# Row statistics of the last spectral tiles moved to where the rows are made, and other places for steps of the attention

## The chip, the cores and the metric

The kernel runs on one core of a Trainium2 chip. The time is device microseconds of that core, the median of the runs shown. Its engines appear under the profile's names: PE is the matrix engine (PEld its weight loads), DVE the vector engine, ACT the scalar engine with the exponentials, POOL the general engine, and SP issues the transfers.

## The reference, cut to what matters

Four layers work on `x` of 2048 rows and 512 columns in f32, each as `x + layer(layernorm(x))`: a spectral layer, an attention layer, then both once more.

```python
def spectral(x):
    a = einsum("bsd,ed->bse", x, dft_hid_re); b = einsum("bsd,ed->bse", x, dft_hid_im)
    return einsum("ts,bse->bte", dft_seq_re, a) - einsum("ts,bse->bte", dft_seq_im, b)

def attention(x, wq, wk, wv, wo, beta):      # 32 heads of 16, 4 segments of 512 rows
    for s in range(4):
        p = softmax(qs @ ks.T * scale + causal_mask)
        a_mem = (phi(qs) @ M) / (phi(qs) @ z + 1e-6)   # memory of the segments before
        o = g * a_mem + (1 - g) * (p @ vs)
        M = M + phi(ks).T @ vs;  z = z + sum(phi(ks))  # phi(t) = t + 1 for t > 0, else exp(t)
    return concat(o) @ wo
```

Both layers begin with a layernorm, which needs a mean and a variance of each row of what the layer before wrote.

## The kernel before, in words

Rows are worked in 16 tiles of 128 rows (`tt`, `i`), four to a segment. The program is the two spectral layers and the two attentions, woven together at their seams. Between them, x goes through DRAM tiles `mid`.

**The spectral layer** multiplies the normalised rows with the DFT matrices (tiles `m`, then `u`, then `y`), the matrices streamed from HBM into a ring (`cring`). Where row tiles are finished, `finish` (L234) adds the residual into `xr` and writes `mid`. For the first three quarters of the rows `measure` (L267) then takes the mean and the variance (`moments`, L195, the statistics at L197) from `xr`, which is still in the chip. When the four tiles of a segment are measured, it turns the variances into row scales: `ve` on DVE, a power on POOL (L210), three small DVE steps `rt` and `row_r` (L215 to L218). The last four tiles, of segment 3, are finished by `hidden_last` (L648), which measures nothing; `prep` of segment 3 reads them back (`xt<-mid`, L185) and does the same statistics there, in the middle of the attention.

**The attention** goes through 32 units, 8 to a segment, 4 heads each (units 0 to 31 in the first attention, and the second attention's are counted 32 to 63 here). A unit has these pieces:

- `nat`: score tiles with rows on the partitions, in pieces of 512, 128+384, 512, 128+384 and 256 columns. DVE takes the maxima of their rows (`junk`, `mx`, L969) and makes `mparts`; PE transposes these (`mT`), ACT copies them (`mt`), and a transfer puts them beside the stacked q (`stkq<-mt`, L1007), so that the next score product subtracts them.
- `sT`: transposed score tiles; ACT reads them (`sT`, L1040; `pT`, L1043 with the exponential), POOL masks the diagonal (L1046).
- `pv_bank`: the value products, 32 columns of PE at a time, at the beginning of a unit as the trace shows it.
- `on`, `oT`: the output transposed to rows and, per row tile, back to columns (`transpose_out`), copied out by ACT and DVE (`oh`, L141).
- `pm` and `pM`, `pkT`: reading the memory (`mem_read`; DVE then does `den`, L1177 and L1185, and `onat`, L1187) and updating it (`mem_update`).
- projections (`pqk`, `pvv`) of the next segment and the output projection (`po`) of the segment before. These run as pairs of half-height products: two tiles, a fixed number of steps apart, each using 64 of PE's rows (`chain_step`). Each unit has 24 of these steps, and `WIN` spreads them over three stretches of the unit.

All PSUM tiles of one bank come from a ring of eight, so a new one waits until the tile of eight before has been read.

**What sets the order.** Each piece is a generator. `place(order, gen, times)` (L250) puts it into a table of slots; ten slots make a unit. At the end the table is worked off by time and then by `order`, and each step records its instructions. PE's order is exactly this program order. On DVE, ACT, POOL and SP a scheduler chooses with the program order as priority; the maxima are given a higher priority. The table's numbers are constants at the top of the file: `S_AT` for the `sT` steps, `N_AT` for `nat`, `PV`, `TO` and `TURN` for value products, output and maxima; `WIN` for the pairs; `ORDER` for the tile that joins each place of the chain; `OT_AT`, `PREP_AT`, `READ_AT`, `UPA` and `UPB` for the unit of a segment in which a transpose, a normalisation, a memory read and the two halves of an update come. The first and the last segment have numbers of their own (`_FIRST`, `_LAST`), and `NL0` says from which unit of the last segment `nat` goes by the last segment's. `ROWS_AT` are the slots in which the second spectral layer loads and normalises its rows, relative to its start.

Of the kernel before, what the change touches and what calls it, by code (L numbers as in the profile page):

```python
# [22 lines left out]
NSEG = 4  # L23
# [4 lines left out]
LT = L // P  # L28
# [13 lines left out]
VW = DH + 1  # L42
HALF = NT // 2
URGENT = 150
S_AT = (1.0, 2.5, 3, 6.0, 7.5)
N_AT = (-17, -15.05, -12, -10.95, -8.0, -8)
PV = 11.05
PVF = 12
W = 2.5
TURN = -5  # L50
TO = 0.8
TURNED = (12.5, 12.5, 14)
WIN = ((4.1, 9), (6.1, 7), (8.1, 8))
LAGS = 18
ORDER = "k3 q3 o1 o0 o2 o3 k0 q0 v2 q1 k1 k2 v1 q2 v3 v0"
OT_AT = (1, 1, 1, 2)
PREP_AT = (2, 3)
READ_AT = (0, 3, 5, 7)
UPA = (-1, 3, 5, 7)
UPB = (4, 4, 6, 8)  # L60
ORDER_FIRST = "q3 k3 - - - - v2 k0 q0 k2 q1 k1 v1 q2 v3 v0"
PREP_FIRST = (2, 3)
UPA_FIRST = (1, 2, 4, 7)
UPB_FIRST = (2, 7, 8, 8)
ORDER_LAST = "k3 q3 o2 o0 - o3 - o1 - - - - - - - -"
OT_LAST = (1, 3, 1, 1)
READ_LAST = (1, 3, 5, 6)
NL0 = 1
SL0 = 2
TURN_LAST = -5  # L70
TURNED_LAST = (12.5, 12.5, 14)
TO_LAST = 1.9
ROWS_AT = (-32, -24, -6, 2, 26, 26, 46, 66)
S_LAST = (0.5, 2.5, 3, 6.0, 7)
N_LAST = (-16.5, -14.05, -13, -11.5, -10.4, -8)
PV_LAST = 10.5
OWO = 0.8
OWU = 0.6
OWP = 0.3
OWR = 0.2  # L80
OWB = 0.3
STK = -21.5
# [15 lines left out]
def spectral_infini_kernel(  # L98
# [155 lines left out]
    def run_from(t, n, step=1):  # L254
        return range(t, t + n * step, step)
# [18 lines left out]
    def place_spectral(x_in, x_out, t0, end, ln_at, direct):  # L274
# [373 lines left out]
        def hidden_last(tcn):  # L648
# [18 lines left out]
            for tt in range(LT):  # L667
                finish(ps[tt], xr[tt], x_out, tcn * LT + tt)
            yield

        for n, t in ln_at:
            measured = t - (1.5 if n[0] == HALF and direct else 3)
# [64 lines left out]
        for tcn in range(TC):  # L737
            if tcn == 0:
                at = [end + k // 2 for k in range(nh)]
            elif tcn < TC - 1:  # L740
                at = [end + nh // 2 + ((tcn - 1) * nh + k) // 3 for k in range(nh)]
            else:
                at = run_from(end + nh // 2 + 2 * nh // 3 + 1, 2 * DT, 2)
            for tt in range(LT):
                place(3.7, split_u(tcn, tt), [at[tt * 2 * DT if tcn < TC - 1 else 0] - 4])
            place(4, (hidden if tcn < TC - 1 else hidden_last)(tcn), at)

    def place_attention(x_in, x_out, t0, w_at, out_at):
# [3 lines left out]
        def prep(s, n):  # L752
# [1 line left out]
            yield  # L754
            mine = slice(s * LT + n[0], s * LT + n[-1] + 1)
            mv, rr = row_mv[:, mine], row_r[:, mine]
            if s == NSEG - 1:
                ve, r = row_stats(xt, mv)
            yield
            if s == NSEG - 1:  # L760
                row_scale(rr, ve, r)
                yield
            xn = []
            for j, i in enumerate(n):
                with behind_max():
# [580 lines left out]
        for s in range(NSEG):  # L1346
            b = t0 + SS * s
            for j in range(2):
                t = b - 43 + 5 * j if s == 0 else apart(s - 1, (PREP_AT if s > 1 else PREP_FIRST)[j])
                first = (12, 10, 6, 4, 3) if s == NSEG - 1 else (11, 8, 5, 3) if s else (8, 5, 4, 3)  # L1350
                place(OWP, prep(s, (2 * j, 2 * j + 1)), [*(t - d for d in first), t, t + 1] if s == 0 else [*(t - d for d in first), t])
            if s == 0:
                place(2, values(s), run_from(b - 18, 8), light(b - 10))
                chain.update({k - 4: chain_proj(0, 2, n) for k, n in ((2, "q"), (3, "k"))})
            at = 2 * USEG * s
            for i in range(LT):
                if s > 0:
# [2 lines left out]
            for name in (ORDER_FIRST if s == 0 else ORDER if s < NSEG - 1 else ORDER_LAST).split():  # L1360
                n, i = name[0], int(name[1:] or 0)
                if n == "-":
                    order.append(None)
                elif n == "o":
                    order.append(chain_out(s - 1, i))
                elif n == "v":
                    order.append(chain_values(s + 1, i))
                else:
                    order.append(chain_proj(s + (i < 3), i, n))
            chain.update({at + h: tile for h, tile in enumerate(order) if tile})  # L1370
# [154 lines left out]
```

## Time and profile before

| | |
|---|---|
| median of three runs | 1778.73 us (1775.21 to 1781.76) |
| profiled execution, and its span | 1775.0 us, 1773.2 us |
| PE busy | 1723.8 us, 97% |
| DVE, ACT, POOL busy | 74%, 62%, 28% |
| mean granted clock of PE | 0.990 |
| first spectral layer, to about | 470 us |
| first attention | 475 to 914 us |
| second spectral layer, to about | 1345 us |
| second attention | 1345 us to the end |

"Busy" of PE is modelled from pipelined matmuls, so a PE that is busy by the page may still work slower than it could. The page's clock line gives the granted clock in tenths. A row of busy time by stretch gives the stretch in us, its length, and for each engine the busy time and the number of instructions, then the granted clock, the share of the transfer engines in use and the rate in GB/s.

### The profile page before, as it was taken

The page shows a single profiled execution, that of the slowest core. Times are in us where ns is not written, and L with a number is a line of the kernel's source. Part 1 is how long each engine was busy: PE and PEld are TensorE (multiplying, and loading weights), DVE is VectorE, ACT ScalarE, POOL GpSimd, SP SyncE. Part 2 cuts the span into 40 slices and gives each one's busy share as a digit, 9 for nine tenths or more (in the row PEclk, how much of TensorE's full clock was granted, in tenths as well). Part 3 has the DMA queues.
Part 4 walks back from the last instruction along what each step waited for, and adds up shares of the span by engine and source line. Part 5 has one row for each costly group of instructions (what it writes and reads, how often), then busy time and mean ns, then how long its engine had stood idle before and what let it go on. Part 6 is the DMA issues. An engine that isn't in the chain of part 4 may idle for free.

```text
span 1773.2 us, 35306 instructions
## 1 busy us (share of the span) xinstructions
PE 1723.8 (97%) x11504; PEld 1341.4 (76%) x11504; DVE 1314.6 (74%) x3949; ACT 1095.5 (62%) x2452; POOL 489.5 (28%) x769
## 2 busy tenths in 40 slices
PE   8999999999999999999999999999999999999998
PEld 6888777877668777777678878888876777777775
DVE  8888978863676876868877997667637667677685
ACT  3344443532588888787764666444418887987885
POOL 1000000003236465455410000000034544754542
PEclk9999999999999999999899999999999999999999
DMA  8787774355455554665656877554555446546551
GB/s 285 248 274 236 250 243 167 103 178 166 125 150 147 134 145 119 159 154 132 178 188 204 277 226 241 193 165 125 171 162 161 123 109 163 146 120 161 135 141 36
DMA packets 145511, 303.29 MB, mean 171 GB/s; under 512 B 18096, under 2 KB 22192, under 8 KB 145328
## 3 DMA queue, kind: packets, MB, share of 16 engines
q1 hardware_dynamic: 138416, 288.44, 54.9%
q10 hardware_dynamic: 6912, 12.59, 1.9%
q8 instruction: 93, 1.52, 0.4%
q14 instruction: 90, 0.74, 0.2%
HBM read 211.83 MB, written 88.08 MB: 169 GB/s over the span
## 4 chain that ended last, share of the span: by engine, by line
PE 78%; DVE 12%; ACT 4%; issue 3%; DMA 2%; POOL 0%; SPq 0%; DVEq 0%; ACTq 0%; POOLq 0%
PE m L124 26%; PE pqk L124 9%; PE y L124 8%; PE pv_bank L124 8%; PE nat L124 5%; PE u L124 5%; PE pvv L124 5%; PE po L124 4%; PE sT L124 4%; DVE junk L969 2%; DVE c L591 2%; DVE clo L141 1%; ACT pT L1043 1%; PE pM L124 1%; PE on L124 1%
## 5 line engine op out<-in xcount | busy, mean ns | idle before, releaser
L969 DVE CUSTOM_DVE_ANT_0 junk<-nat,mask 128x128 bf16<-128x128 f32 (+3 forms) x896 | 368.9, 457 | 231.6 <-PE nat L124 217.4
L1043 ACT ACTIVATE pT<-sT 128x512 f32<-128x512 f32 x640 | 353.1, 607 | 3.3 <-DVE sT L1038 1.1
L124 PE MATMUL m<-chi,xa 128*128 128x512 f32 x1056 | 308.3, 392 | 2.4 <-DVE c L591 2.1
L1046 POOL TENSOR_SCALAR_AFFINE_SELECT pT<-pT 128x256 f32<-128x256 f32 (+1 forms) x448 | 193.2, 446 | 399.8 <-ACT pT L1043 329.3
L124 PE MATMUL m<-clo,xa 128*128 128x512 f32 x720 | 231.8, 394 | 4.7 <-DVE clo L141 4.4
L124 PEld LDWEIGHTS m<-chi,xa 128*128 128x128 f32 x1056 | 198.0, 188 | 47.0 <-DVE c L591 2.9
L1040 ACT ACTIVATE sT<-sT 128x256 f32<-128x256 f32 x625 | 181.8, 329 | 80.4 <-PE sT L124 74.8
L124 PE MATMUL nat<-stkk,stkq 48*128 48x384 f32 (+3 forms) x1024 | 197.3, 354 | 12.3 <-PE sT L124 3.4
L124 PE MATMUL pqk<-xT,wq 64*128 64x512 f32 (+1 forms) x720 | 193.7, 399 | 0.8 <-ACT pT L1043 0.6
L124 PE MATMUL pqk<-xT,wk 64*128 64x512 f32 (+1 forms) x720 | 188.3, 398 | 0.3
L124 PE MATMUL y<-wdt,us 128*128 128x512 f32 x768 | 182.3, 391 | 0.2 <-DVE wdt L141 0.2
L124 PE MATMUL pvv<-wv,xT 64*128 64x512 f32 (+1 forms) x672 | 173.2, 402 | 0.5 <-DVE xT L141 0.4
L124 PEld LDWEIGHTS nat<-stkk,stkq 48*128 48x128 f32 x1024 | 122.6, 187 | 65.8 <-ACT pT L1043 19.3
L124 PE MATMUL sT<-stkq,stkk 50*128 50x256 f32 (+3 forms) x1024 | 165.6, 334 | 5.9 <-DMA stkq<-mt 2.7
L124 PEld LDWEIGHTS y<-wdt,us 128*128 128x128 f32 x768 | 143.4, 188 | 30.5 <-DVE wdt L141 0.9
L124 PEld LDWEIGHTS m<-clo,xa 128*128 128x128 f32 x720 | 134.7, 188 | 37.8 <-DVE clo L141 8.9
L124 PE MATMUL pv_bank<-pT,v_all 128*32 128x512 f32 (+3 forms) x2048 | 162.5, 452 | 0.2 <-DVE xr L235 0.2
L139 ACT ACTIVATE chi<-cring 128x512 fp32r<-128x512 f32 (+1 forms) x138 | 99.7, 727 | 88.0 <-PE m L124 40.1
L210 POOL TENSOR_TENSOR r<-ve,half_neg 128x2 f32<-128x2 f32 (+2 forms) x24 | 19.7, 819 | 481.3 <-DVE ve L208 457.5
L124 PE MATMUL po<-wo,oh 64*128 64x512 f32 (+1 forms) x672 | 147.7, 401 | 1.1 <-ACT oh L139 0.5
L124 PEld LDWEIGHTS pqk<-xT,wq 64*128 64x128 f32 (+1 forms) x720 | 123.9, 187 | 13.4 <-issue 2.2
L124 PEld LDWEIGHTS sT<-stkq,stkk 50*128 50x128 f32 x1024 | 105.5, 188 | 37.3 <-issue 12.4
(191 smaller groups left out, 3134.5 us busy)
## 6 DMA issues: line engine op xcount, KB each, us to landing
cring<-in_ct SPq DMA_DIRECT2D x97, 256.0 KB
scrk<-parts SPq DMA_DIRECT2D x96, 256.0 KB
stkq<-scrq SPq DMA_DIRECT2D x128, 192.0 KB
stkk<-scrk SPq DMA_DIRECT2D x128, 192.0 KB
cring<-sum SPq DMA_DIRECT2D x95, 256.0 KB
xt<-mid SPq DMA_DIRECT2D x64, 256.0 KB
scrq<-parts SPq DMA_DIRECT2D x32, 512.0 KB
cring<-in_ct SPq DMA_DIRECT2D x27, 512.0 KB
```

The lines of the kernel that those rows point to most:

```text
L124: return tc.keep_in_program_order(op(*args, **kwargs))
L139: pin(A.activation(hi, src, AF.Copy, scale=scale))
L141: lo_engine.tensor_tensor(out=lo, in0=src, in1=hi.bitcast(F32), op=ALU.subtract)
L210: G.tensor_tensor(out=r, in0=ve, in1=half_neg[:, :n], op=ALU.pow)
L591: V.tensor_tensor(out=dst, in0=c[tcn, base][:, m], in1=ps[m], op=op)
L969: last_max[0] = V.tensor_tensor_reduce(trash, src, mask[:, 512 - n :], 1.0, 3e38, ALU.add, ALU.min, dst,)
L1040: done = A.activation(blocks, blocks, AF.Relu)
L1043: A.activation(dst[a], ps, AF.Exp, scale=-SCALE)
L1046: G.affine_select(blocks, blocks, pattern=[[0, n] for n in blocks.shape[1:-1]] + [[1, P]], compare_op=ALU.is_ge, fill=0.0, base=0, channel ...
```

## The change

The last spectral tiles are measured in `hidden_last`, in four steps that are placed after its end, and `prep` of segment 3 does no statistics any more: the four `moments` per seam go from `xt` to `xr`, and their scales are made once for four tiles rather than twice for two. The two projections ahead of the chain are named by a constant `ORDER_PRE`, and `ORDER` may now name tiles "Q" and "K", which none of the lists does. All else are numbers of the table. Lines of the changed file stand one further from L43 on.

```diff
-S_AT = (1.0, 2.5, 3, 6.0, 7.5)
-N_AT = (-17, -15.05, -12, -10.95, -8.0, -8)
-PV = 11.05
+S_AT = (1.0, 2.5, 3, 5.5, 7.5)
+N_AT = (-16.05, -15.1, -12.05, -10.95, -8.0, -8)
+PV = 11.9
...
-TO = 0.8
+TO = 0.75
-WIN = ((4.1, 9), (6.1, 7), (8.1, 8))
+WIN = ((4.1, 10), (6.1, 6), (8.1, 8))
...
-READ_AT = (0, 3, 5, 7)
-UPA = (-1, 3, 5, 7)
-UPB = (4, 4, 6, 8)
-ORDER_FIRST = "q3 k3 - - - - v2 k0 q0 k2 q1 k1 v1 q2 v3 v0"
+READ_AT = (1, 3, 5, 7)
+UPA = (-1, 3, 3, 7)
+UPB = (4, 5, 6, 8)
+ORDER_PRE = "q2 k2"
+ORDER_FIRST = "q3 k3 - - - - v2 k0 q0 q1 k1 k2 v0 q2 v3 v1"
...
-UPA_FIRST = (1, 2, 4, 7)
+UPA_FIRST = (1, 2, 4, 5)
...
-OT_LAST = (1, 3, 1, 1)
+OT_LAST = (1, 2, 1, 1)
...
-NL0 = 1
+NL0 = 0
...
-TO_LAST = 1.9
-ROWS_AT = (-32, -24, -6, 2, 26, 26, 46, 66)
-S_LAST = (0.5, 2.5, 3, 6.0, 7)
-N_LAST = (-16.5, -14.05, -13, -11.5, -10.4, -8)
-PV_LAST = 10.5
+TO_LAST = 0.8
+ROWS_AT = (-38, -24, -12, 2, 26, 28, 40, 66)
+S_LAST = (1.5, 2.5, 3, 6.0, 6)
+N_LAST = (-15.55, -14.05, -12.5, -11.0, -10.9, -8)
+PV_LAST = 11.5
...
-OWP = 0.3
+OWP = 0.4
...
             for tt in range(LT):
                 finish(ps[tt], xr[tt], x_out, tcn * LT + tt)
             yield
+            for tt in range(LT):
+                measure(tcn, tt, xr[tt])
+                yield
...
                 at = run_from(end + nh // 2 + 2 * nh // 3 + 1, 2 * DT, 2)
+                at = [*at, *(at[-1] + 4 + k for k in range(LT))]
...
-            if s == NSEG - 1:
-                ve, r = row_stats(xt, mv)
-            yield
-            if s == NSEG - 1:
-                row_scale(rr, ve, r)
-                yield
+            yield
...
-                first = (12, 10, 6, 4, 3) if s == NSEG - 1 else (11, 8, 5, 3) if s else (8, 5, 4, 3)
+                first = (11, 8, 5, 3) if s else (8, 5, 4, 3)
...
-                chain.update({k - 4: chain_proj(0, 2, n) for k, n in ((2, "q"), (3, "k"))})
+                for k, name in enumerate(ORDER_PRE.split()):
+                    if name != "-":
+                        chain[k - 2] = chain_proj(0, 2, name[0].lower())
...
+                elif n in "QK":
+                    order.append(chain_proj(s, i, n.lower()))
```

What this does to the order of the instructions shows at three places.

DVE in unit 17, where statistics for segment 3 stood before; the rows begin behind the four maxima of 256 columns.

```order
L1133 TENSOR_TENSOR rec<-on,gate 128x16
L988 TENSOR_SCALAR mparts_70<-mx 128x2x8
L1139 RECIPROCAL rec<-rec 128x16
L989 SCALAR_TENSOR_TENSOR mparts_70<-mx,mparts_70 128x2x8
L197 BN_STATS st<-xt 128x6
L1150 TENSOR_TENSOR ot<-on,rec 128x256
L198 BN_AGGR row_mv<-st 128x2
L197 BN_STATS st<-xt 128x6
L141 TENSOR_TENSOR oh<-oT,oh 128x512 x2
L969 ISA junk,mx<-nat,mask 128x512
```

The same place of the changed kernel:

```order
L1177 SCALAR_TENSOR_TENSOR den<-pm,gate 128x16
L988 TENSOR_SCALAR mparts_70<-mx 128x2x8
L1177 SCALAR_TENSOR_TENSOR den<-pm,gate 128x16
L989 SCALAR_TENSOR_TENSOR mparts_70<-mx,mparts_70 128x2x8
L1185 RECIPROCAL den<-den 128x32
L1133 TENSOR_TENSOR rec<-on,gate 128x16
L1187 TENSOR_TENSOR onat<-pm,den 128x2x128 x2
L1139 RECIPROCAL rec<-rec 128x16
L142 TENSOR_TENSOR oh<-oT,oh 128x512
L1150 TENSOR_TENSOR ot<-on,rec 128x256
L142 TENSOR_TENSOR oh<-oT,oh 128x512 x2
L969 ISA junk,mx<-nat,mask 128x512
```

The statistics are gone from here; the work of the memory read (`den`, `onat`) and the third `oh` now stand ahead of the maximum of the first 512 columns.

PE at the beginning of unit 8 before, where the first memory read of segment 1 stood:

```order
L124 MATMUL nat<-stkk,stkq 128x256 x4
L124 MATMUL sT<-stkq,stkk 128x384 x2
L124 MATMUL sT<-stkq,stkk 128x128 x2
L124 MATMUL pm<-state_4422,phi 128x136 x4
L124 MATMUL pM<-v_all,pkn 128x136 x8
L124 MATMUL on<-ident,ot 128x128 x4
```

and at the beginning of unit 9 in the changed kernel:

```order
L125 MATMUL nat<-stkk,stkq 128x256 x4
L125 MATMUL sT<-stkq,stkk 128x384 x2
L125 MATMUL sT<-stkq,stkk 128x128 x2
L125 MATMUL pm<-state_4443,phi 128x136 x4
L125 MATMUL on<-ident,ot 128x128 x4
L125 MATMUL oT<-ident,onat 128x128 x12
```

The read stands one unit later, ahead of the three transposes of the output. The same holds for units 16 and 17, 40 and 41, 48 and 49.

SP near the end of the first attention, around the transfer of the transposed maxima (`stkq<-mt`), before:

```order
L416 DMA cring<-in_ct 128x512 x2
L236 DMA mid_9_140<-xr 128x512
L416 DMA cring<-in_ct 128x512 x6
L185 DMA xt<-mid_8_139 128x512
L1007 DMA stkq<-mt 2x8x128 x2
L185 DMA xt<-mid_9_140 128x512
L185 DMA xt<-mid_10_141 128x512
```

and changed:

```order
L417 DMA cring<-in_ct 128x512 x4
L237 DMA mid_9_140<-xr 128x512
L417 DMA cring<-in_ct 128x512 x4
L186 DMA xt<-mid_8_139 128x512
L186 DMA xt<-mid_9_140 128x512
L186 DMA xt<-mid_10_141 128x512
L1007 DMA stkq<-mt 2x8x128 x2
```

Two loads of spectral rows have come ahead of it.

## The prediction

> **What bounds the kernel now.** I read the page from the top: busy shares, slices in time, the chain.
>
> ```profile
> span 1773.2 us, 35306 instructions
> PE 1723.8 (97%) x11504; PEld 1341.4 (76%) x11504; DVE 1314.6 (74%) x3949; ACT 1095.5 (62%) x2452; POOL 489.5 (28%) x769
> PEclk9999999999999999999899999999999999999999
> PE 78%; DVE 12%; ACT 4%; issue 3%; DMA 2%; POOL 0%; SPq 0%; DVEq 0%; ACTq 0%; POOLq 0%
> ```
>
> PE is the bound: busy 1723.8 of 1773.2 us, and 78% of the chain. All its idle time is 49.4 us, and the change removes no matmul, so it can win only idle time, time at a lower clock, and matmuls that are stretched by what they wait for. So I compared units of one kind in the view of busy time by stretch (length; busy us of PE, PEld, DVE, ACT, POOL, each with its count; clock; DMA share; GB/s): three output units of segment 2 beside those of segment 3, in attention 1 and 2, and behind them the same four stretches for L197, the statistics of a row tile, alone.
>
> ```profile
> 581.86:625.91 44.05, 42.56 (x403) 32.17 (x406) 37.44 (x135) 34.31 (x86) 19.80 (x33) 1.00 0.51 140
> 695.34:741.40 46.06, 42.93 (x402) 30.84 (x406) 40.05 (x153) 35.26 (x86) 21.34 (x35) 1.00 0.52 135
> 1453.60:1497.60 44.00, 42.51 (x402) 32.06 (x406) 34.82 (x131) 34.33 (x86) 19.80 (x33) 1.00 0.52 141
> 1566.84:1612.99 46.15, 42.53 (x403) 31.78 (x406) 38.51 (x151) 35.06 (x87) 21.46 (x35) 1.00 0.51 132
> ...
> 581.86:625.91 44.05, 2.50 (x4) 1.00 0.51 140
> 695.34:741.40 46.06, 5.16 (x8) 1.00 0.52 135
> 1453.60:1497.60 44.00, 0.00 (x0) 1.00 0.52 141
> 1566.84:1612.99 46.15, 2.69 (x4) 1.00 0.51 132
> ```
>
> PE has the same number of matmuls in all four, yet units 17 to 19 and 49 to 51 take 2.01 and 2.15 us longer than units 9 to 11 and 41 to 43. What they have beyond the others is four statistics of xt (2.69 us, 0.67 each) and what hangs on them: `prep` of segment 3 computes its row scales there, because the rows come too late for the segment before. The chain of waits runs through that work in unit 17 and again in unit 18 (start, us):
>
> ```profile
> 704.81 0.74 POOL r L210
> ...
> 706.62 0.51 DVE rt L217
> ...
> 707.87 0.50 PE sT L124
> ...
> 718.46 0.60 DVE st L197
> ...
> 720.36 0.58 DVE st L197
> ```
>
> DVE works in its order; the maxima (junk) that free the banks of `nat` stand behind these pieces, and PE waits for a bank.
>
> **The change, part by part.** The sum is made against the profiled execution's 1775.0 us.
>
> *Row statistics where the rows are made.* The statistics leave units 17 to 19 and 49 to 51. If these then run as their twins, that is −2.01 −2.15 = **−4.1**. Bounds: no gain, if the pace was set by something else there, and −4.1. The twins have the same PE instructions, so I take −4.1.
>
> The four statistics go to the lead of each attention, where the last row tiles are finished. The first row is DVE's busy time in the lead, the second the first maximum after it, with the idle time ahead of it:
>
> ```profile
> 446.70:458.58 11.88, 5.87 (x30) 1.00 0.41 140
> ...
> 458.58 0.69 DVE L969 CUSTOM_DVE_ANT_0 junk<-nat,mask 128x512 bf16<-128x512 f32 x1 [4.89 <-PE nat L124]
> ```
>
> DVE is idle for 4.89 us just where the moved work (4×0.67 = 2.7 and small pieces) comes. Without that cover PE would wait for the maxima: +2.7 in the first lead. The order puts the first statistic between maxima that PE waits for, so I take one of the four as uncovered: **+0.6**, bounds 0 and +2.7.
>
> *First memory read from units 8, 16, 40, 48 to 9, 17, 41, 49.* In units 8 and 16 nothing of it is hidden, PE is dense there; in 9 and 17 PE waits later for the transposed output. Unit 25 already has the order that unit 9 now gets: read, `on`, twelve `oT`. So I compare both from the value products to the first `po`, PE's timeline first, then the chain in unit 25, then DVE's timeline in unit 9:
>
> ```profile
> 570.23 1.19 PE L124 MATMUL pm<-state,phi 128*128 128x136 f32 x8
> 571.26 2.02 PE L124 MATMUL pM<-v_all,pkn 128*128 128x136 f32 x16
> ...
> 581.79 2.36 PE L124 MATMUL pv_bank<-pT,v_all 128*32 128x512 f32 x32
> ...
> 588.46 0.47 PE L124 MATMUL po<-wo,oh 64*128 64x512 f32 x1 [0.20 <-DVE mx L969]
> ...
> 807.15 2.36 PE L124 MATMUL pv_bank<-pT,v_all 128*32 128x512 f32 x32
> ...
> 814.29 0.50 PE L124 MATMUL po<-wo,oh 64*128 64x512 f32 x1
> ```
>
> ```profile
> 811.77 0.75 DVE onat L1187 x2
> ...
> 813.63 0.61 DVE oh L141
> ```
>
> ```profile
> 587.63 0.68 DVE L969 CUSTOM_DVE_ANT_0 junk<-nat,mask 128x512 bf16<-128x512 f32 x1
> ...
> 588.23 1.28 DVE L141 TENSOR_TENSOR oh<-oT,oh 128x512 fp32r<-128x512 f32 x2
> ```
>
> The read takes 571.26 − 570.23 = 1.03 us of PE and leaves unit 8. In unit 9 the way to the first `po` is 588.46 − 581.79 = 6.67 us, in unit 25 it is 814.29 − 807.15 = 7.14, though unit 25 has no `nat` of 256 columns there. So the read adds at least 0.47 in its new place. It adds more where those tiles stand too, since DVE then comes from their maxima, does `onat` (0.75) and `oh`, and only then lets `po` start; I take 0.9 of the 1.03. Four units times −0.13 is **−0.5**; the end on the good side is 4×−1.03 = −4.1 (wholly hidden), the bad one is the fourth rival's.
>
> *Output transpose from unit 27 to 26, `nat` steps of units 22 to 25 and 54 to 57 in the order of the last units, earlier spectral rows.* Rows of busy time by stretch: units 22 to 25, 26 to 28, 29; then two windows of 3.41 us at the half-clock piece, and one for comparison.
>
> ```profile
> 768.49:822.12 53.63, 53.42 (x528) 41.05 (x532) 38.82 (x172) 45.35 (x115) 27.46 (x46) 1.00 0.52 133
> 822.12:859.10 36.98, 34.99 (x292) 24.97 (x293) 32.20 (x126) 28.43 (x76) 23.26 (x38) 0.95 0.61 157
> 859.10:872.23 13.13, 9.71 (x83) 6.02 (x86) 12.87 (x58) 9.50 (x26) 4.91 (x10) 0.89 0.98 286
> ...
> 838.75:842.16 3.41, 2.64 (x15) 1.69 (x14) 3.31 (x12) 3.41 (x10) 3.33 (x4) 1.00 0.43 122
> 842.16:845.57 3.41, 3.41 (x19) 2.91 (x19) 2.45 (x11) 2.68 (x7) 2.23 (x7) 0.50 0.33 117
> 698.80:702.21 3.41, 2.40 (x19) 1.75 (x17) 3.41 (x16) 3.41 (x9) 1.64 (x4) 1.00 0.00 0
> ```
>
> Units 22 to 25 have 0.21 us of idle PE, so their new order can hardly win; it puts two chain pairs ahead of `nat`, and a `po` that waits for `oh` then waits without `nat` as filler. Two pairs are 814.63 to 814.86, twice, 0.46 us:
>
> ```profile
> 814.63 0.39 PE L124 MATMUL po<-wo,oh 64*128 64x512 f32 x1
> ...
> 814.86 0.39 PE L124 MATMUL po<-wo,oh 64*128 64x512 f32 x1
> ```
>
> `nat` of 512 columns is itself late by a wait in some of these units and by none in others. I take 0, bounds 8×0.46 = +3.7 and, where `nat` no longer waits, half of that as a gain, −1.8.
>
> Units 26 to 28 lose 36.98 − 34.99 = 1.99 us idle and 3.41/2 = 1.7 at half clock; both come together in unit 27, where the transpose, a read and a normalised spectral row meet. The transpose goes to unit 26 and the row to an earlier slot. I take **−1.5**, bounds −3.7 and +1 (the same stall in unit 26).
>
> [...]
>
> *End of attention 1.* The transfer of the transposed maxima (mt) for the last `sT` now stands behind two more 256 KB loads on SP. The chain's row of it, and SP's row of those two loads:
>
> ```profile
> 865.95 5.04 DMA stkq<-mt
> ...
> 868.38 1.95 SPq L185 DMA_DIRECT2D xt<-mid  x2
> ```
>
> PE waits for this transfer. Two loads take 1.95 us to issue, and 512 KB at that unit's 286 GB/s take 1.8 us. Part goes by while earlier loads drain: **+1**, bounds 0 and +2.
>
> *At nothing.* `sT` one pair (0.23 us) earlier: the exponentials behind it wait for ACT, which works at 34.31 of 44.05 us and has the same order. Key update and state steps that change units take their PE time along. The lead's projections are the same tiles at the same chain places as before: nothing moves.
>
> Sum: −4.1 + 0.6 − 0.5 − 1.5 + 1 = **−4.5**, so 1770.5 for the profiled execution. The median of the runs is 1778.73 (1775.21 to 1781.76), 3.7 above it: **1774**.
>
> **The rivals.** [...]
>
> *Nothing to measure*: the pace of units 17 to 19 is set by the banks, whatever DVE does, and the gain of the statistics goes to a quarter: 1774 + 3.1 = 1777. For it: the read fills the very DVE places that the statistics leave in unit 17 (the order above). [...]
>
> *DVE late, slower*: in units 9, 17, 41 and 49 `onat` (0.75) and two more `oh` (1.28) now stand ahead of the first maximum: 2.0 us, 8.1 in all. With 0.46 in each of the eight units with late `nat` (3.7) and without the read's −0.5 it is 1774 + 12.3 = 1786. It decides where the maximum comes later than the bank is wanted, some 2.3 us (ten pairs) after its matmul. For it: the order. Against it: DVE has 10.36 us of work in a unit of 14.68, and catches up:
>
> ```profile
> 581.86:596.54 14.68, 14.14 (x132) 10.01 (x132) 10.36 (x44) 13.10 (x33) 7.68 (x12) 1.00 0.37 98
> ```
>
> *The change does less than its words*: the joined projections move nothing. That is in the sum.
>
> **How the numbers follow.** The forecast has 0.52, more than the sum 0.22, nothing 0.14, slower 0.12. Half a per cent, what a measurement of this kernel can tell, is 8.9 us: under 1769.8 or over 1787.6. The forecast's own range is 1768 to 1780, a tenth of it below the bound. Faster: 0.05 + 0.22 + 0.03 (ends of the terms together) = 0.30. Slower: 0.05 of the slower case, and 0.05 for an order that stalls where the trace has no twin. Same: 0.60. The range goes to both outer cases: 1763 to 1786.
>
> **What would show it.** Units 17 to 19 and 49 to 51 at 44 us, with no L197 (now L198) on xt: right on the statistics. A chain through `onat` and `oh` in units 9, 17, 41, 49, or these at over 15.7 us with 8 and 16 at 13.5: the slower rival. No half clock at 842: the term on unit 27. A gap ahead of `sT` in unit 29 beyond 5.04 us: the transfer. The prediction is wrong if units that I count at nothing (4 to 8, 22 to 25) change by over half a microsecond each.

## The result, and the profile after

The changed kernel takes 1762.92 us (median of four runs, 1758.46 to 1766.95), the kernel before 1778.03 beside it. The ratio is 0.9918, with a 95% interval of 0.9893 to 0.9943: 14.6 us less, between 10 and 19. That is faster by more than the half per cent at which I drew the line. The forecast was 1774, with a range from 1763 to 1786: the sign is right, the size about a third of what came, and the time lies at the range's lower edge, 0.1 us outside it.

The page of the changed kernel (span, busy time, granted clock, chain by engine):

```profile
span 1761.5 us, 35311 instructions
...
PE 1719.8 (98%) x11504; PEld 1347.1 (76%) x11504; DVE 1315.4 (75%) x3939; ACT 1092.1 (62%) x2452; POOL 489.6 (28%) x767
...
PEclk9999999999999999999999999999999999999999
...
PE 79%; DVE 10%; ACT 4%; DMA 3%; issue 3%; POOL 0%; SPq 0%; DVEq 0%; ACTq 0%; POOLq 0%
```

PE's idle time has gone from 49.4 to 1761.5 − 1719.8 = 41.7 us. DVE's part of the chain has gone from 12% to 10%.

To see where the time went I cut both traces at the first value product of each unit. Two executions of one kernel agree there within 0.05 us in most units. The stretches in which the prediction found the statistics are now (busy time by stretch, units 9 to 11, 17 to 19, 41 to 43, 49 to 51; then L198, the statistics, alone):

```profile
582.35:627.20 44.85, 43.67 (x413) 34.64 (x411) 38.37 (x140) 34.90 (x87) 19.81 (x33) 1.00 0.53 138
695.38:740.18 44.80, 43.63 (x413) 34.07 (x411) 38.31 (x140) 34.93 (x87) 19.77 (x33) 1.00 0.51 139
1445.86:1490.64 44.78, 43.60 (x413) 33.33 (x411) 35.81 (x136) 34.94 (x87) 19.76 (x33) 1.00 0.53 138
1558.87:1603.70 44.83, 43.68 (x413) 33.79 (x411) 35.73 (x136) 34.95 (x87) 19.79 (x33) 1.00 0.52 137
...
582.35:627.20 44.85, 2.42 (x4) 1.00 0.53 138
695.38:740.18 44.80, 2.42 (x4) 1.00 0.51 139
1445.86:1490.64 44.78, 0.00 (x0) 1.00 0.53 138
1558.87:1603.70 44.83, 0.00 (x0) 1.00 0.52 137
```

The four are equal now, within 0.07 us. All of them hold one memory read more than before, which is why units 9 to 11 went up from 44.05 to 44.85 (with the read taken back, below, they are at 44.03).

### The profile page after: what moved, and what is told of

Read it like the earlier page. It is cut to its first block, busy times and chain, and to the rows that moved or that the text cites. A ratio compares the mean times of both kernels' runs of the same rounds, so it can differ in the third digit from the quotient of the medians.

```text
span 1761.5 us, 35311 instructions
## 1 busy us (share of the span) xinstructions
PE 1719.8 (98%) x11504; PEld 1347.1 (76%) x11504; DVE 1315.4 (75%) x3939; ACT 1092.1 (62%) x2452; POOL 489.6 (28%) x767
## 4 chain that ended last, share of the span: by engine, by line
PE 79%; DVE 10%; ACT 4%; DMA 3%; issue 3%; POOL 0%; SPq 0%; DVEq 0%; ACTq 0%; POOLq 0%
PE m L125 25%; PE pqk L125 9%; PE y L125 8%; PE pv_bank L125 8%; PE nat L125 6%; PE u L125 5%; PE pvv L125 5%; PE po L125 5%; PE sT L125 4%; DVE junk L969 2%; DVE c L592 2%; DVE clo L142 1%; PE pM L125 1%; ACT pT L1043 1%; PE pm L125 1%
## 5 line engine op out<-in xcount | busy, mean ns | idle before, releaser
L125 PE MATMUL pqk<-xT,wk 64*128 64x512 f32 (+1 forms) x720 | 193.8, 398 | 0.2
L211 POOL TENSOR_TENSOR r<-ve,half_neg 128x4 f32<-128x4 f32 (+2 forms) x22 | 20.8, 945 | 510.4 <-DVE ve L209 486.5
L125 PEld LDWEIGHTS pqk<-xT,wk 64*128 64x128 f32 (+1 forms) x720 | 122.8, 186 | 12.2 <-issue 2.2
```

The costliest lines, as they stand in the source:

```text
L125: return tc.keep_in_program_order(op(*args, **kwargs))
L211: G.tensor_tensor(out=r, in0=ve, in1=half_neg[:, :n], op=ALU.pow)
```

## The experiments

Each kernel is the one before or the changed one with one part exchanged. "Stretches" below are cut at the value products. All ratios are to the kernel before, run beside it, with 95% intervals.

| kernel | ratio | profiled span, us | mean clock |
|---|---|---|---|
| changed kernel | 0.9918 (0.9893 to 0.9943) | 1761.5 | 0.989 |
| before + statistics moved | 0.9959 (0.9944 to 0.9974) | 1764.9 | 0.991 |
| before + read moved | 1.0022 (1.0003 to 1.0041) | 1785.4 | 0.980 |
| before + steady units' numbers | 0.9987 (0.9971 to 1.0004) | 1774.2 | 0.988 |
| before + last units' numbers | 0.9986 (0.9973 to 0.9999) | 1771.6 | 0.988 |
| before + row slots | 1.0001 (0.9988 to 1.0014) | 1775.5 | 0.986 |
| before + update places | 1.0004 (0.9991 to 1.0018) | 1769.9 | 0.991 |
| before + statistics twice | 1.0038 (1.0024 to 1.0053) | 1780.5 | 0.990 |
| changed, statistics not moved | 0.9942 (0.9928 to 0.9957) | 1766.2 | 0.989 |
| changed, read moved back | 0.9930 (0.9914 to 0.9946) | 1762.9 | 0.990 |
| changed, maxima ahead of the loads | 0.9923 (0.9907 to 0.9938) | 1761.5 | 0.989 |
| changed, transpose back in unit 27 | 0.9933 (0.9916 to 0.9950) | 1759.9 | 0.991 |
| before, once more | one run, 1774.51 us | 1772.7 | 0.990 |

### The statistics alone

```diff
+            for tt in range(LT):
+                measure(tcn, tt, xr[tt])
+                yield
...
+                at = [*at, *(at[-1] + 4 + k for k in range(LT))]
...
-            if s == NSEG - 1:
-                ve, r = row_stats(xt, mv)
-            yield
-            if s == NSEG - 1:
-                row_scale(rr, ve, r)
-                yield
+            yield
...
-                first = (12, 10, 6, 4, 3) if s == NSEG - 1 else (11, 8, 5, 3) if s else (8, 5, 4, 3)
+                first = (11, 8, 5, 3) if s else (8, 5, 4, 3)
```

> The kernel before with the moved row statistics alone. If the statistics set the pace of units 17 to 19 and 49 to 51 (the prediction's first term), these two stretches take about 44.0 us instead of 46.06 and 46.15, all other units stay within 0.2 us, and the time falls by 4 us, less at most 0.6 in the leads. If the banks set the pace and the statistics only filled it (the rival in which nothing is to measure), the stretches stay above 45.3 us and the time within 2 us of the kernel before.

Units 17 to 19 and 49 to 51 of this kernel, by stretch:

```profile
692.95:737.52 44.57, 42.57 (x401) 32.25 (x399) 37.67 (x135) 34.74 (x86) 19.76 (x33) 1.00 0.53 138
1561.46:1605.52 44.06, 42.56 (x400) 32.39 (x398) 34.86 (x131) 34.31 (x86) 19.73 (x33) 1.00 0.51 140
```

46.06 became 44.57 and 46.15 became 44.06, with PE's work the same: 3.6 us in all. The second stretch reaches its twin's 44.00; the first stays half a microsecond above it. The statistics and what hangs on them set the pace, not the banks whatever DVE does. The timed ratio says 7.3 us, with an interval from 4.6 to 9.9, so more than the stretches show.

### The statistics made twice

```diff
             if s == NSEG - 1:
+                row_stats(xt, mv)
                 ve, r = row_stats(xt, mv)
```

> The kernel before with each statistic and its mean in segment 3's normalisation made twice, so four more statistics of 0.67 us for each attention. If DVE's work there sets the pace, as taking it away showed (46.06 to 44.57 and 46.15 to 44.06 us), units 17 to 19 and 49 to 51 become 1.5 to 2.7 us longer each, and the time rises by 3 to 5 us. If only the chain behind the statistics (power, small steps, normalisation) did it, they rise by under 0.7 us.

```profile
696.97:748.25 51.28, 44.87 (x400) 31.80 (x398) 45.10 (x163) 35.31 (x86) 22.46 (x37) 1.00 0.46 119
1570.75:1620.90 50.15, 44.38 (x400) 31.86 (x398) 43.04 (x159) 35.19 (x86) 22.45 (x37) 1.00 0.45 123
```

The stretches went up by 5.2 and 4.0 us, one and a half to two times the most that I expected from the added work on DVE (four statistics of 0.67 us, 2.7 us); the time rose by 6.8 us (4.3 to 9.4). What I had not counted: calling the function twice also makes the power on POOL twice, and the second power with what follows it comes a good deal later. Powers on POOL in this stretch (tile `r`, L210), with what waits for them:

```profile
L210 POOL TENSOR_TENSOR r<-ve,half_neg x4: 702/714/730, 706.5 to 729.9; 128x2 f32<-128x2 f32 x4
L215 DVE TENSOR_TENSOR rt<-r x2: 348/798/1249, 710.1 to 730.6; 128x2 f32<-128x2 f32 x2
```

The same in the kernel before:

```profile
L210 POOL TENSOR_TENSOR r<-ve,half_neg x2: 731/731/731, 704.8 to 722.4; 128x2 f32<-128x2 f32 x2
L215 DVE TENSOR_TENSOR rt<-r x2: 150/156/161, 705.6 to 723.6; 128x2 f32<-128x2 f32 x2
```

The first scale step comes at 710.1 − 697.0 = 13.1 us after the stretch began, and at 705.6 − 695.3 = 10.3 in the kernel before. So the run doubled the chain from the statistics to the row scale along with DVE's work, and the stretches answered more than in proportion. How much of it is DVE's time and how much the two waits isn't separated here, so the run does not decide between the two readings that were expected of it.

### The read alone, and the read taken back

```diff
-READ_AT = (0, 3, 5, 7)
+READ_AT = (1, 3, 5, 7)
```

> The kernel before with the first memory read moved alone (units 8, 16, 40, 48 to 9, 17, 41, 49). By the prediction's term units 8 and 16 lose 1.0 us each and 9 and 17 gain 0.8 to 0.9: -0.1 to -0.2 for a pair of units, -0.5 in all. If the read is hidden, unit 9 stays at 14.7 us and the time falls by 4. If DVE comes too late (the slower rival), units 9 and 17 gain 2 us and the time rises by 4; in unit 17 the statistics still stand in DVE's way here, so it would show there first.

The other way round, in the changed kernel:

```diff
-READ_AT = (1, 3, 5, 7)
+READ_AT = (0, 3, 5, 7)
```

> The changed kernel with the first memory read back in units 8, 16, 40 and 48. By the units of the two profiles the move is worth 0.2 us for each pair, 0.8 in all: units 8 and 16 at 14.5 and 13.6 us, 9 and 17 at 14.7 us, and a time within 2 us of the changed kernel (0.991 to 0.993 of the kernel before). If the move costs what it cost alone (0.22% more than before), this kernel is 4 us faster than the changed one and the best so far.

Units 8 and 9, then 16 and 17, of the changed kernel:

```profile
568.82:597.83 29.01, 28.69 (x275) 22.22 (x273) 19.99 (x89) 23.71 (x60) 14.36 (x21) 1.00 0.45 111
682.79:710.86 28.07, 27.75 (x266) 21.48 (x265) 19.46 (x86) 23.52 (x59) 15.14 (x23) 1.00 0.44 110
```

and with the read taken back:

```profile
567.15:596.32 29.17, 28.65 (x274) 22.00 (x272) 20.22 (x89) 23.55 (x60) 14.34 (x21) 1.00 0.45 112
681.44:709.66 28.22, 27.70 (x265) 21.30 (x264) 19.48 (x86) 23.32 (x60) 14.99 (x23) 1.00 0.45 109
```

The move is worth 0.16 and 0.15 us for these two pairs, 0.17 and 0.34 for the other two: 0.8 in all, against a forecast of 0.5. The chain of the changed kernel in unit 9 is the one that the prediction read from unit 25:

```profile
586.65 0.09 DVE den L1177
...
587.44 0.76 DVE onat L1187 x2
...
588.35 0.55 DVE oh L142
588.90 0.33 DVE ot L1150
589.22 0.61 DVE oh L142
...
589.88 0.49 PE po L125
```

From the value products at 582.35 to the first `po` it is now 7.53 us; it was 6.67. The read costs 0.86 in its new place (forecast 0.9) and saves 1.0 in the old one.

In the kernel before, the read met the statistics: units 16 to 19 went from 59.63 to 60.12 us, while in the changed kernel they take 57.39.

```profile
681.26:741.38 60.12, 57.53 (x534) 44.29 (x533) 50.94 (x197) 45.52 (x113) 28.68 (x47) 1.00 0.52 129
```

There the move does not win 0.15 us but costs 0.5. In units 48 to 51, beside the other attention's statistics, it costs nothing (59.68 us against 59.75). The ratio of 1.0022 (3.9 us more) has another source: this kernel's profile has more pieces at half clock than that of the kernel before, one of them in unit 43, where nothing was changed. The lost clock, one minus the mean clock times the span, is some 35 us against 18. The timed runs show the same. Their mean is 5.1 us above the mean of the kernel before, and the lost clock, worked out for each run from its own span and clock, is 26.7 us on average against 21.5, which is 5.2 more. So the read by itself costs little; why this kernel gets more time at half clock stays open.

### The numbers of the steady units alone

```diff
-S_AT = (1.0, 2.5, 3, 6.0, 7.5)
-N_AT = (-17, -15.05, -12, -10.95, -8.0, -8)
-PV = 11.05
+S_AT = (1.0, 2.5, 3, 5.5, 7.5)
+N_AT = (-16.05, -15.1, -12.05, -10.95, -8.0, -8)
+PV = 11.9
...
-TO = 0.8
+TO = 0.75
...
-WIN = ((4.1, 9), (6.1, 7), (8.1, 8))
+WIN = ((4.1, 10), (6.1, 6), (8.1, 8))
```

> The kernel before with the numbers of the steady units alone (score steps S_AT and N_AT, PV, TO, WIN). The prediction counted the earlier score step at nothing: all units from 4 to 21 and 36 to 53 within 0.1 us of before, the time within 2 us. If the earlier step feeds ACT sooner, the units with a wait for the exponential (5, 6, 9, 12, 14) lose up to 0.5 us each and the time falls by some 5 us.

Units 4 to 16 stayed within 0.15 us each, the time within what can be told. The units with a wait for the exponential gained nothing: an earlier `sT` is worth nothing there, as forecast. Beside the statistics single units moved by more than the expected 0.1 us, by up to 0.7: units 17 to 19 took 46.53 us and 49 to 51 45.73, where the kernel before has 46.06 and 46.15. Unit 18 holds a piece at half clock here.

### The update places alone

```diff
-UPA = (-1, 3, 5, 7)
-UPB = (4, 4, 6, 8)
+UPA = (-1, 3, 3, 7)
+UPB = (4, 5, 6, 8)
...
-ORDER_FIRST = "q3 k3 - - - - v2 k0 q0 k2 q1 k1 v1 q2 v3 v0"
+ORDER_FIRST = "q3 k3 - - - - v2 k0 q0 q1 k1 k2 v0 q2 v3 v1"
...
-UPA_FIRST = (1, 2, 4, 7)
+UPA_FIRST = (1, 2, 4, 5)
```

> The kernel before with the memory updates and the first segment's tiles alone at their new places (UPA, UPB, UPA_FIRST, ORDER_FIRST). The prediction counted them at nothing. By the changed kernel's profile units 5 and 37 gain 0.5 us, 7 and 39 lose 0.5, 12 and 13 together lose 0.3; the sum is within 0.5 us, the time within 2 us of before. If the places of the updates are worth what the steady units can't explain, the time falls by 3 or more.

Unit 5 became 0.56 us longer and unit 7 0.48 shorter; 12 became 0.56 shorter and 13 0.20 longer; 20 became 0.52 shorter and 21 0.21 longer. The state step moved from unit 12 to 13 and from 20 to 21 leaves something, about 0.3 a time. Unit 18 became 1.4 us longer here, where the statistics still stood, and the timed ratio is 1.0004. So alone it is worth nothing.

### The numbers of the last units alone

```diff
-OT_LAST = (1, 3, 1, 1)
+OT_LAST = (1, 2, 1, 1)
...
-NL0 = 1
+NL0 = 0
...
-TO_LAST = 1.9
+TO_LAST = 0.8
...
-S_LAST = (0.5, 2.5, 3, 6.0, 7)
-N_LAST = (-16.5, -14.05, -13, -11.5, -10.4, -8)
-PV_LAST = 10.5
+S_LAST = (1.5, 2.5, 3, 6.0, 6)
+N_LAST = (-15.55, -14.05, -12.5, -11.0, -10.9, -8)
+PV_LAST = 11.5
```

> The kernel before with the numbers of the last units alone (transpose in unit 26 instead of 27, score steps, value products and outputs of the last segment). The changed kernel's profile has units 22 to 25 0.8 us shorter, 26 to 29 2.0, 30 and 31 1.4, and in the second attention 1.1, 0.7 and 0.1. If these numbers cause it, they come back here within 0.3 us each and the time falls by about 6. If the earlier spectral rows or the moved statistics cause what units 26 to 31 win, only units 22 to 25 are shorter here, by 0.8 and 1.1, and the time falls by about 2.

Units 22 to 25 and 54 to 57 of this kernel:

```profile
770.31:822.79 52.48, 52.28 (x522) 40.03 (x520) 40.08 (x168) 45.12 (x114) 27.45 (x46) 1.00 0.52 134
1640.50:1693.02 52.52, 52.32 (x523) 40.03 (x521) 39.93 (x168) 45.13 (x114) 27.50 (x46) 1.00 0.50 131
```

53.63 and 53.95 became 52.48 and 52.52, so these numbers are the cause of what those units won (52.80 and 52.82 in the changed kernel). Four `sT` products that belong to these stretches come just behind their end here, so this kernel's rows show a little too much; the changed kernel has the same matmuls in the stretch as the one before. Its rows, and those of the second profile of the kernel before:

```profile
767.25:820.05 52.80, 52.60 (x526) 40.43 (x524) 40.26 (x168) 45.28 (x115) 27.69 (x46) 1.00 0.53 136
1630.63:1683.45 52.82, 52.62 (x526) 40.59 (x524) 40.09 (x168) 45.24 (x115) 27.73 (x46) 1.00 0.51 131
...
769.55:823.28 53.73, 53.53 (x527) 40.89 (x525) 38.81 (x170) 45.40 (x114) 27.37 (x46) 1.00 0.52 133
1639.27:1693.25 53.98, 53.72 (x527) 41.66 (x525) 39.07 (x172) 45.80 (x114) 27.36 (x46) 1.00 0.50 134
```

PE's idle time is the same, 0.20 us in each row but the last (0.26). What got shorter is busy time, the same matmuls in less of it.

Unit 31 became 0.39 us shorter (0.43 in the changed kernel), unit 59 1.1. Units 26 to 29 did not get shorter here, so what unit 27 wins in the changed kernel has another cause. The time fell by 2.5 us (0.2 to 4.8), as the second of the two readings expected.

Where the gain in unit 25, and likewise in unit 57, comes from is seen in the changed kernel's chain:

```profile
810.16 0.76 DVE onat L1187 x2
810.92 0.16 DVE rec L1139
811.08 0.62 DVE oh L142
811.70 0.14 issue
811.84 0.47 PE po L125
...
812.57 0.60 PE nat L125 x2
```

`po` now stands ahead of `nat` on PE, and DVE makes the `oh` that `po` needs first: `po` starts 6.30 us after the value products, not 7.14. I had argued as if DVE's order stayed, and `po` would wait without `nat` as filler. But the scheduler sets DVE's order from the order in which the program needs things. This is 0.4 of the 0.9 us in units 22 to 25, and 0.6 of 1.2 in units 54 to 57. Most of the rest lies in units 22 and 23, 54 and 55, where no `po` waits: in unit 23 the first two `nat` matmuls of 512 columns stood directly behind `sT` and kept the next matmul off for 0.51 us (786.47 to 786.98 in the first profile of the kernel before), and behind two pairs they take 0.24 (785.81 to 786.05 in the changed kernel). Why they are slower in the one place is not shown.

### The row slots alone, and the kernel before a second time

```diff
-ROWS_AT = (-32, -24, -6, 2, 26, 26, 46, 66)
+ROWS_AT = (-38, -24, -12, 2, 26, 28, 40, 66)
...
-OWP = 0.3
+OWP = 0.4
```

> The kernel before with the spectral rows alone at their new slots (ROWS_AT, and the weight of the normalisation). If unit 27's half-clock piece and length (14.56 us) come from the normalised row that meets the transpose and the read there, unit 27 falls to about 12.0 us without the transpose being moved, and the time falls by 2 to 3 us. If the transpose is the cause, unit 27 stays at 14 us or more. The transfer of the maxima behind two more loads makes unit 29 longer by up to 2 us, by the prediction's term 1 us.

> The kernel before once more, for a second profile. Its first profile has a time of 1775.0 us against a median near 1776.5 to 1778. Units without a wait for transfers should repeat within 0.05 us; unit 38 (14.83 us, against 13.4 to 13.9 in all other profiles) should come out at 13.4 to 14.0, and the pieces at half clock at about the same places, with some more or fewer of 3.4 us.

Unit 27 with the new row slots, and unit 29:

```profile
836.05:848.27 12.22, 11.71 (x107) 9.02 (x107) 10.99 (x47) 9.19 (x25) 5.07 (x11) 1.00 0.65 151
857.89:871.53 13.64, 10.86 (x79) 7.25 (x78) 13.55 (x59) 10.53 (x28) 5.81 (x10) 0.78 0.88 268
```

The same two units of the kernel before in its second profile:

```profile
835.61:848.80 13.19, 12.39 (x107) 9.09 (x106) 12.86 (x49) 10.28 (x26) 8.58 (x14) 1.00 0.62 156
858.79:870.64 11.85, 9.21 (x79) 5.63 (x78) 11.60 (x54) 9.54 (x26) 4.88 (x10) 0.93 0.93 276
```

and of the changed kernel:

```profile
833.24:845.06 11.82, 11.07 (x103) 8.33 (x103) 11.08 (x50) 8.53 (x24) 4.94 (x11) 1.00 0.58 142
854.75:868.16 13.41, 10.90 (x79) 7.12 (x78) 13.36 (x57) 10.47 (x28) 4.89 (x10) 0.84 0.88 269
```

In the second profile of the kernel before, the half-clock piece in unit 27, on which a term of the prediction rested, is not there: the clock is 1.00 and the unit takes 13.19 us where it took 14.55. That alone would make the piece an event of one execution. The other kernels' profiles say otherwise. Unit 27 in all of them, with the time at half clock in it:

| rows at the old slots | unit 27, us | half clock, us | rows at the new slots | unit 27, us | half clock, us |
|---|---|---|---|---|---|
| before | 14.56 | 3.41 | changed kernel | 11.83 | 0 |
| before, once more | 13.20 | 0 | before + row slots | 12.22 | 0 |
| before + statistics moved | 15.84 | 6.83 | changed, statistics not moved | 11.82 | 0 |
| before + read moved | 14.85 | 3.41 | changed, read moved back | 11.83 | 0 |
| before + steady units' numbers | 13.61 | 0 | changed, transpose back | 12.56 | 0 |
| before + last units' numbers | 16.08 | 6.83 | changed, maxima ahead of the loads | 11.82 | 0 |
| before + update places | 14.32 | 3.41 | | | |
| before + statistics twice | 14.45 | 3.41 | | | |

With the old slots six of eight executions have a half-clock piece in unit 27, with the new ones none of six. Whether one comes depends on the execution, but with the new slots none came at all. On average the new slots make unit 27 2.6 us shorter (14.61 against 12.01); against the second profile alone it would be 0.97 us (1.37 in the changed kernel). Unit 38, 14.83 us in the first profile and 13.47 in the second, is at full clock in both; it lies between 13.2 and 14.2 in all other profiles. In unit 29 the new slots lose 1.79 us against the second profile (1.56 in the changed kernel), of which the next section tells more. By time the slots alone are worth nothing that can be told (1.0001, 0.9988 to 1.0014).

### The transfer of the maxima, and the transpose

```diff
-ROWS_AT = (-38, -24, -12, 2, 26, 28, 40, 66)
+ROWS_AT = (-38, -24, -6, 2, 26, 28, 40, 66)
```

> The changed kernel with the third pair of spectral rows back at slot -6, so that the transfer of the maxima stands ahead of the two loads again. By the prediction's term unit 29 (13.42 us) becomes 1 us shorter and the time falls by 1. If the transfer is hidden by the matmuls that run at half clock there (no wait for it shows in the changed kernel), unit 29 changes by under 0.3 us and the time stays.

Unit 29 with the transfer of the maxima again ahead of the two loads:

```profile
854.84:866.97 12.13, 9.82 (x79) 6.44 (x79) 11.98 (x56) 8.51 (x24) 5.02 (x10) 0.86 0.90 258
```

Unit 29 became 1.28 us shorter. Unit 30 took 0.55 back, and the time is the changed kernel's within the intervals. Two executions of the kernel before differ as much in unit 29 (13.1 and 11.9 us), but over all profiles the order holds: 11.9 to 13.1 us in the eight with the old slots, 12.1 here, and 13.4 to 14.0 in the five with all the new ones. The averages are 1.2 us apart, of which 0.6 is time lost at half clock.

So the prediction's number came, but not by its wait. The last `sT` of the unit waited 2.68 us for the transfer in the kernel before, and in the changed kernel it doesn't wait for it (over all profiles, 0 to 0.7 us with all the new slots, and 0.9 to 2.7 in seven of the eight with the old ones):

```profile
871.12 1.10 PE L124 MATMUL sT<-stkq,stkk 50*128 50x256 f32 x4 [2.68 <-DMA stkq<-mt]
...
867.28 0.95 PE L125 MATMUL sT<-stkq,stkk 50*128 50x256 f32 x4 [0.23 <-ACT chi L140]
```

What comes late is the maxima themselves. The copies `mt` that the transfer moves, before and changed, and a row of the changed kernel's chain ahead of them:

```profile
L1004 ACT ACTIVATE mt<-mT x2: 202/204/206, 864.9 to 865.0; 32x64 fp32r<-32x64 f32 x2
...
L1004 ACT ACTIVATE mt<-mT x2: 196/196/196, 862.2 to 863.2; 32x64 fp32r<-32x64 f32 x2
...
858.64 0.92 DVE xn L232 x2
```

Counted from the unit's first value product, the two copies start at 5.8 and 5.9 us in the kernel before, at 7.4 and 8.5 in the changed one, and at 5.9 and 6.3 in this run. The slot that places the loads also places the normalisation of those rows (`xn`) on DVE: it starts 3.8 us into the unit in the changed kernel, ahead of maxima that PE waits for, and at 8.7 in the kernel before and 9.8 in this run. The changed kernel issues the transfer 0.45 us after the second copy has ended, so the loads can hold it up by no more than that. This run moves loads and normalisation together; by the traces it is DVE's order, and not SP's, that costs.

```diff
-OT_LAST = (1, 2, 1, 1)
+OT_LAST = (1, 3, 1, 1)
```

> The changed kernel with the second output transpose of the last segment back in units 27 and 59. The new slots of the rows alone gave 2.3 of unit 27's 2.7 us; so here unit 27 should stay below 12.5 us, unit 59 return from 11.1 to 12.1 us, unit 26 lose the 0.7 us that it gained, and the time stay within 2 us of the changed kernel. If the transpose is what matters in unit 27, it returns to 14 us.

With the transpose back, unit 27 takes 12.56 us and unit 26 12.61, where the changed kernel has 11.82 and 13.19: 25.17 against 25.01. Unit 59 becomes 0.78 us longer (11.90 against 11.12) and unit 58 0.7 shorter. The transpose moves time from one unit to the next; the rows were what mattered in unit 27, which has no piece at half clock in either kernel.

### All but the statistics

The changed kernel with the four edits of the first experiment undone.

> The changed kernel with the statistics left in the normalisation of segment 3 as before; all other numbers changed. The statistics alone gave 0.9959 of the kernel before, some 7 us, of which the units show 4. If their worth is the same here, this kernel stands 4 to 7 us above the changed one (0.995 to 0.996 of the kernel before). If the moved read needs the place that the statistics leave, it stands further above, 10 us or more, since units 17 and 49 then hold both (16.4 us each, as in the kernel with the read moved alone).

```profile
693.33:740.30 46.97, 44.40 (x412) 33.77 (x411) 42.41 (x158) 35.61 (x87) 21.17 (x35) 1.00 0.49 131
1560.25:1606.96 46.71, 44.15 (x412) 33.62 (x411) 40.49 (x154) 35.11 (x87) 21.17 (x35) 1.00 0.51 130
```

Against the changed kernel's 44.80 and 44.83 the statistics cost 2.17 and 1.88 us here, 4.05 together, and the profiled spans differ by 4.7. Their worth is the same with the other numbers changed. But this kernel is 0.58% faster than the one before (0.43 to 0.72), while its parts alone come to 1.0022, 0.9987, 0.9986, 1.0001 and 1.0004, no gain at all in their sum. Much of that gap is granted clock, as the end of the next section works out.

## Why the prediction was right in sign and too small

**Statistics, −4.1: right.** 4.05 us by taking them back, 3.6 by moving them alone. The reading of twin stretches gave it; the rival that nothing would be gained has fallen.

**The lead, +0.6: nothing was lost.** DVE took the four statistics in its gap; the wait ahead of the next maximum shrank from 4.89 to 1.95 us, and PE did not lose by it. From the last `xr` of the spectral layer to that maximum it takes 460.21 − 445.71 = 14.50 us, and 458.58 − 443.96 = 14.62 in the kernel before. The row of DVE's timeline in the lead:

```profile
460.21 0.69 DVE L969 CUSTOM_DVE_ANT_0 junk<-nat,mask 128x512 bf16<-128x512 f32 x1 [1.95 <-PE nat L125]
```

**The read, −0.5: right (−0.8).** Unit 25 was a good twin for the new unit 9. The slower rival's mechanism came, at the size given: the first maximum starts 7.99 us after the value products instead of 5.84. But it decided nothing, as DVE caught up within the unit.

**Transpose and rows, −1.5: right in kind, too small.** The term for unit 27 priced the idle time and the half-clock piece that one execution showed, and took them to go with the row. They did: units 26 to 28 take 37.11 us on average over the eight profiles with the old slots and 34.76 over the five with all the new ones, 2.3 us less. Against the second profile of the kernel before alone it is 0.8, as that one happens to have no piece. How −1.5 was chosen between its bounds of −3.7 and +1 the prediction doesn't say. It was the row and not the transpose that did it, which the prediction had left together.

**`nat` order, 0: the largest miss.** In units 22 to 25 and 54 to 57 it was worth 53.73 + 53.98 − 52.80 − 52.82 = 2.1 us, just past the good end of its bounds. Two steps failed. One is "0.21 us of idle PE, so their new order can hardly win": idle PE stayed at 0.20, and the same matmuls took less busy time, though the prediction itself had named matmuls that are stretched by what they wait for as a thing to win. The other is "a `po` that waits for `oh` then waits without `nat` as filler": `oh` came earlier. By the prediction's own sign of being wrong, units counted at nothing that change by over half a microsecond, it was wrong here (unit 23, 0.6 shorter) and in unit 5 (0.5 longer).

**The maxima behind two loads, +1: the number by luck.** Unit 29 became 1.2 us longer on average, but PE does not wait for the transfer in the changed kernel; the gap beyond 5.04 us that was to show it is not there. The step that failed is the wait: the new slot put the normalisation of the rows on DVE ahead of the maxima, which the prediction did not count.

**At nothing:** right for `sT`; too small for the rest. In the units of the updates between 10 and 53 that no other term covers, the changed kernel's profile is 1.6 us shorter than the second one of the kernel before and, unit 38 left out, 0.7 shorter than the first. That the updates are the cause is shown only where they stood alone, by some 0.3 us in units 12 and 13 and again in 20 and 21. The order of the last products beside the spectral layer wins 0.4 in unit 31.

**More than the sum,** at a chance of 0.22, is what came, though the read was not hidden (0.8 us of 4.1) and of the half-clock pieces only the one in unit 27 went. Nothing that the prediction worked out reaches 1763; where its range begins there, it doesn't say why. Its likeliest outcome, at 0.60, was a change of less than half a per cent.

**The sum.** Cut at the value products, the changed kernel's profile is 11.2 us shorter than the second one of the kernel before: 4.4 in units 16 to 19 and 48 to 51, 2.1 in 22 to 25 and 54 to 57, 0.4 in the other units of the moved read, some 1.5 in the units of the updates, 0.8 lost in units 26 to 29. Another 1.8 lie in units 30 and 31 and 1.2 behind the last unit's start. Of those two only the 0.4 of unit 31 repeat in other kernels with the same edit: unit 30 varies by more than a microsecond with its clock, and the end is also short in kernels that did not change it. So some 8 to 9 of the 11.2 us are the change's. With units 26 to 29 taken over all profiles (49.63 us on average at the old slots, 48.45 at the new) instead of that one, they win 1.2 and don't lose 0.8, and it is about 10. The forecast was 4.5.

**What stays open.** The timed difference, 10 to 19 us, has the profiles' 11.2 in its interval, but the parts' timed ratios don't add: alone they come to −0.4%, together to −0.8%. Most of that is granted clock, which was taken in every timed run. By plain means the six parts come to −4.8 us in sum, and the changed kernel to −14.1 against the 62 runs of the kernel before that were timed beside the parts. With each run's lost clock taken off, they come to −9.9 and −11.2. This is an estimate, as it counts a microsecond of lost clock as one of time; within the runs of one kernel the time rises by about 0.7 per microsecond lost, by which it is −8.4 and −12.0. Two of the parts also lose time next to the statistics in units 17 to 19 when they stand alone (the read, the updates). Why a kernel gets more or fewer pieces at half clock is not shown; that an edit can take one away is shown for unit 27 alone.

The version with the maxima ahead of the loads is better than the changed kernel by 0.7 us in units 29 and 30 of its profile, though not in its span. The one with the transpose back has a span 1.6 us shorter, of which 1.5 lie in unit 32, which that edit doesn't touch. Their ratios of 0.9923 and 0.9933 tell them apart from the kernel before but not from the changed one.

## What to carry to other kernels

Look for two stretches with the same matmuls and different lengths: what the longer one does beyond the other, on whatever engine, is priced by the difference, and here that price held to 0.1 us in the changed kernel and to half a microsecond alone. Before a term rests on an event such as a piece at low clock, look at the same place in many executions: one profile showed the piece, a second didn't, and only all of them together showed that it came in six of eight and went with the change. Little idle time doesn't mean that a stretch can't get shorter: here 53.73 us became 52.80 with 0.20 idle in both. When a run bears out a number, ask the trace whether it was the wait that you named. And when the program's order changes on one engine, ask what a scheduler then does on the others before pricing a wait.

## What the runs showed of the hardware

The pieces at half clock (granted clock 0.50) of 3.4 us come and go between executions of one kernel. The kernel before had one at 842.16 us in one profile and none there in the other, with mean clocks of 0.990 in both. Within each of the 14 traces all starts of such pieces lie whole multiples of 3.413 us apart, to 0.01 us, so each trace has a grid, and it stands at another place in each: its first point in unit 27 comes 0.84 us after the first value product in the first profile of the kernel before and 2.60 in the second. How busy PE was just ahead does not tell a stretch with a piece behind it from one without: in the first profile of the kernel before PE worked for 2.64 of the 3.41 us ahead of the piece at 842.16, and for 2.40 of the 3.41 from 698.80, with the clock at 1.00 in the 3.41 behind them. With the old row slots the six executions with that point at 0.4 to 1.9 us have the piece in unit 27 and the two at 2.6 and 2.8 have none; with the new slots none has it, at points from 0.2 to 3.4.

Work on DVE that PE waits for cost more here than it takes: 2.7 us of added statistics, with two more powers on POOL (0.71 us each), made stretches of three units longer by 5.2 and 4.0 us.

The granted clock goes with most of the scatter between runs of one kernel here: over the 62 runs of the kernel before, time and lost clock have a correlation of 0.88.
